# A linear-attention and feed-forward kernel: products with the state row-tiled over two PSUM banks, the state update issued behind them

## The chip, the cores and the metric

The kernel runs on one core of one Trainium2 chip. The metric is the time of one execution in microseconds (us); of the kernel before there are three runs with a median of 691.35 us (689.48 to 691.96). One more execution was taken with the hardware profiler.

## The reference

Three stages follow one another; everything is float32.

```python
# 1 attention with a decaying state: batch 4, 8 heads, 768 steps, head size 48
for t in range(S):
    state = alpha[:, :, t, :, None] * state + np.einsum('bhd,bhe->bhde', k[:, :, t], v[:, :, t])
    y[:, :, t] = np.einsum('bhd,bhde->bhe', q[:, :, t], state)
x = y.transpose(0, 2, 1, 3).reshape(B, S, 384)
# 2 gated feed-forward with a convolution of three taps over time: 384 -> 1024 -> 384
h = np.maximum(x @ w_in, 0.0)
conv_out = conv_w[0] * h[t - 1] + conv_w[1] * h[t] + conv_w[2] * h[t + 1]
x = (h * sigmoid(conv_out)) @ w_out
# 3 layer norm and feed-forward with a residual: 384 -> 1536 -> 384
xn = (x - mu) / np.sqrt(var + 1e-06) * g_ln
out = x + np.maximum(xn @ w_ch1, 0.0) @ w_ch2
```

## The kernel before, in words

Time is cut into 24 chunks of 128 steps (six to a batch, chunks 0, 6, 12 and 18 begin one) and 12 blocks of 256 steps (two chunks each). A chunk is the unit of stage 1, a block that of stages 2 and 3.

**A chunk.** The eight heads stand in four pairs p; the first head of a pair (g = 0) lies on SBUF partitions 0 to 47, the second (g = 1) on 64 to 111 (`rows`). The decays are turned into running products on VectorE (lines 399 and 415), and `a` holds q times the decay, `later` k times its inverse. TensorE (PE) then makes, in this order:

- the scores `s` of all heads (line 441), two PSUM banks, one for each g; the two g work in different halves of the array's rows. VectorE masks them into `pm` (line 450, twice).
- `kt`, four transposes of k (line 465), one bank; ScalarE copies it to `kts` (line 469). The last chunk of a batch leaves `kt` and the update out.
- the outputs `y` (line 509), one bank with four strips of 32 partitions and three column ranges k of 128 steps. The products with the state come first (12, and none in a batch's first chunk), then 16 products of v with `pm`. Each output is 32 features wide, so that four products with four strips stand side by side. In the products with the state (`state[:, p, ...]`, all 112 partitions) both heads of a pair are in the rows: 8 products give the first 32 features of a head (k = 0 and 1), 4 the last 16 of both heads (k = 2).
- the update `u` (line 525), a step of its own with a bank of its own: 8 products of 64 or 48 columns, which VectorE adds to `state` (lines 534 and 536). GpSimd multiplies the state by its decay before the next chunk (line 482).

`evict_x` empties `y`: ScalarE rounds it into `xh` (line 556, one instruction of 128x384) and VectorE writes the rest `xl` (line 562, one instruction). The feed-forward stages work on such pairs of a rounded part and a rest: three products for each one of the reference, at lines 595 (`h`, stage 2, from `xh`, `xl`), 790 (`h`, stage 3) and 687 (`acc`, the second product of both).

**Order.** All instructions are recorded as steps with an estimated cost, and a planner (`Plan.order`) simulates the five engines' queues with these costs, the buffers' rings and due times, and emits the steps in the order that comes out; every engine then runs its list in order. In the first 150 us the weights are converted too (lines 254 to 312: from 64-bit floats, by ScalarE, VectorE, then PE or GpSimd; the tiles `z`, `w`, `low`). From chunk 3 on, all of a chunk's banks come from one ring of two (`att_bank`, tag `att`); chunks 0 to 2 use another ring of three (`acc`).

At the end the kernel reads a flag and, where some decay was out of range, would run a general version (`general`, `general_x`); it isn't run with these inputs.

Of the kernel before, what the change touches and what calls it, by code (L numbers as in the profile page):

```python
# [26 lines left out]
K1 = DM // 128  # L27
# [189 lines left out]
def attn_moe_kernel(ctx: ExitStack, tc, qka, vv, qka_t, v_t, w_in, conv_w, w_out, g_ln, w_ch1, w_ch2, out):  # L217
    nc = tc.nc
    pe, act, dve, pool, sp = nc.tensor, nc.scalar, nc.vector, nc.gpsimd, nc.sync
    plan = Plan()  # L220
    add, ring = plan.add, plan.ring
# [253 lines left out]
    def att_pe2(c):  # L475


        u, t = att[c], {}
        first, last = c % NCB == 0, c % NCB == NCB - 1
        if not first:  # L480
            def decay():
                pool.tensor_tensor(
                    out=state, in0=state,
                    in1=ends[:, c].rearrange("r (p o) -> r p o", o=1).to_broadcast([R, NP, 2 * D]), op=ALU.mult,
                )

            add("pool", pool_us(NP * 2 * D), decay, r=[("ends", c)], w=[("state", 0)], port=True)
        b0 = att_bank(c)

        def outputs():  # L490
            qd, v, pm = prep[c]["qd"], vraw[c], post[c][0]
            ps = t["y"] = bank(b0[0], "y")
            products = []
            if not first:
                for k in range(2):
                    for n in range(4):
                        p, g = divmod(4 * k + n, 2)
                        products.append((k, n, state[:, p, state_mains[g]], qd[:, NP - 1 - p, :]))
                for p in range(NP):
                    products.append((2, p, state[:, p, 32:64], qd[:, NP - 1 - p, :]))  # L500
            for k in range(2):
                for n in range(4):
                    p, g = divmod(4 * k + n, 2)
                    products.append((k, n, v[:, p, mains[g]], pm[:, g, p, :]))
            for g in range(2):
                for p in range(NP):
                    products.append((2, p, v[:, p, rests[g]], pm[:, g, p, :]))
            for m, (k, n, l, r) in enumerate(products):
                pe.matmul(  # L509
                    out=ps[32 * n:32 * n + 32, k * C:(k + 1) * C], lhsT=l, rhs=r,  # L510
                    start=m < 4, stop=m >= len(products) - 4, skip_group_check=True,
                )

        reads = [u["v"], u["pm"], u["a"]] + ([] if first else [("state", 0)])
        add("pe", 0.9 if first else 1.5, outputs, r=reads, new=[b0[1]], mode="cols")
        evict_x(c, t, b0[1])
        if last:
            return
        b1 = att_bank(c)

        def update():
            ps, kts, v = bank(b1[0], "u"), post[c][1], vraw[c]
            for p in range(NP):
                for g, w in enumerate(wide):
                    pe.matmul(  # L525
                        out=ps[w, p * D:(p + 1) * D], lhsT=kts[:, p, w], rhs=v[:, p, wholes[g]], start=True, stop=True,
                    )
            t["u"] = ps[:, :NP * D].rearrange("r (p e) -> r p e", p=NP)

        def add_up():  # L530
            for g, r in enumerate(rows):
                st = state[r, :, blocks[g]]
                if first:
                    dve.tensor_copy(out=st, in_=t["u"][r])
                else:
                    dve.tensor_tensor(out=st, in0=t["u"][r], in1=st, op=ALU.add)

        add("pe", 0.4, update, r=[u["kts"], u["v"]], new=[b1[1]], mode="halves")
        add("dve", 2 * dve_us(NP * D), add_up, r=[b1[1]], w=[("state", 0)])

    def evict_x(c, t, b):

        i, half = divmod(c, NT)
        first, last = i % (S // T) == 0, i % (S // T) == S // T - 1
        new = half == 0
        if new:
            x_b[i] = [ring(f"x{s}", XB) for s in "hl"]
        cols = slice(1 + half * C, 1 + (half + 1) * C)

        def source():  # L550
            return t["y"][:, :DM].rearrange("f (k t) -> f k t", k=K1)

        def high():
            if new:
                x_t[i] = [wk.tile([128, K1, T + 2], F32R, tag="xh", name="xh", bufs=XB), None]
            act.activation(out=x_t[i][0][:, :, cols], in_=source(), func=ACTF.Copy)

        def rest():
            if new:
                x_t[i][1] = wk.tile([128, K1, T + 2], F32R, tag="xl", name="xl", bufs=XB)  # L560
            hi, lo = x_t[i]
            dve.tensor_tensor(out=lo[:, :, cols], in0=source(), in1=hi[:, :, cols], op=ALU.subtract)

        def sides():
            for n, x in enumerate(x_t[i]):
                if new and first:
                    pool.memset(x[:, :, 0:1].bitcast(F32), 0.0)
                if new and not first:
                    before = x_t[i - 1][n]
                    pool.tensor_copy(out=x[:, :, 0:1], in_=before[:, :, T:T + 1])  # L570
                    pool.tensor_copy(out=before[:, :, T + 1:T + 2], in_=x[:, :, 1:2])
                if half == NT - 1 and last:
                    pool.memset(x[:, :, T + 1:T + 2].bitcast(F32), 0.0)

        bh, bl = x_b[i]
        add("act", act_us(DM), high, r=[b], **{"new" if new else "w": [bh]})
        add("dve", dve_us(DM), rest, r=[b, bh], **{"new" if new else "w": [bl]})
        if new or (half == NT - 1 and last):
            add("pool", 0.3, sides, w=[bh, bl] + (x_b[i - 1] if new and not first else []))

# [317 lines left out]
    def general_x(xs, b, t0):  # L898

        hi, lo = x_t[0] = [wk.tile([128, K1, T + 2], F32R, tag=f"x{s}", name=f"x{s}", bufs=1) for s in "hl"]  # L900
        for t, n in [(t, 128) for t in range(0, T, 128)] + [(T, 2)]:
            rowf = wk.tile([128, DM], F32, tag="row", name="row")
            split = 32 * H
            src = xs[bass.ds(b, 1), bass.ds(t0 + t, n)].rearrange("o t g (p e) -> (o t) g p e", e=D)
            for part, es in ((rowf[:n, :split], slice(0, 32)), (rowf[:n, split:], slice(32, D))):
                for g in range(2):
                    sp.dma_start(
                        out=part.rearrange("t (p g e) -> t p g e", p=NP, g=2)[:, :, g, :], in_=src[:, g, :, es]
                    )
            ps = psum.tile([128, 512], F32, tag="h", name="h", bufs=HB)  # L910
            for k in range(K1):
                pe.transpose(ps[:, k * 128:k * 128 + n], rowf[:n, k * 128:(k + 1) * 128], ident[:n, :n])
            src = ps[:, :DM].rearrange("p (k t) -> p k t", k=K1)[:, :, :n]
            act.activation(out=hi[:, :, t:t + n], in_=src, func=ACTF.Copy)
            dve.tensor_tensor(out=lo[:, :, t:t + n], in0=src, in1=hi[:, :, t:t + n], op=ALU.subtract)
# [35 lines left out]
    begin, n = {}, 0  # L951
# [75 lines left out]
    for s, i, part in up:  # L1027
        m = begin[s, i, part]
# [61 lines left out]
def _layout(inputs):  # L1090
# [34 lines left out]
    for n in ("moe_w_in", "moe2_w_ch1"):  # L1125
        w = inputs[n]
        if n == "moe_w_in":
            w = w.reshape(H, D, -1)
            w = np.concatenate([w[:, :32].reshape(32 * H, -1), w[:, 32:].reshape(DM - 32 * H, -1)])
        w = w.reshape(K1, 128, -1, 128)  # L1130
        weights[n] = w.transpose(2, 1, 0, 3).reshape(-1, 128, DM)
    for n in ("moe_w_out", "moe2_w_ch2"):
# [25 lines left out]
```

## Time and profile before

| | us |
|---|---|
| median of three runs | 691.35 |
| the profiled execution | 688.87 |
| its span, first to last instruction | 687.1 |
| PE busy (matmul) | 643.6 |
| VectorE (DVE) busy | 449.5 |
| ScalarE (ACT) busy | 308.8 |
| GpSimd (POOL) busy | 127.1 |

PE is the engine that is busy in nearly all of the span. A matmul of float32 operands leaves two records in the trace, one of the rounded operands (`fp32r`) one. [...] PEclk is the clock granted to PE, 1.00 for 2.4 GHz and 0.50 for 1.2 GHz.

### The profile page before, as it was taken

How to read it: one execution, taken by the hardware profiler on the slowest of the kernel's cores; microseconds unless marked ns; L12 is line 12 of the kernel's file. 1: busy time of each engine (PE TensorE's matmuls, PEld its weight loads, DVE VectorE, ACT ScalarE, POOL GpSimd, SP SyncE). 2: the span in 40 equal slices, each digit the busy share in tenths (PEclk: the TensorE clock that was granted, in tenths of full speed). 3: DMA queues.
4: the chain of work that ended last, by engine and by line, in shares of the span. 5: the costliest groups of instructions: out<-in, count | busy, mean ns of one | idle time of the engine just before them, and what ended most of it. 6: DMA issues, size and time to landing. Idle time of an engine off the chain costs nothing.

```text
span 687.1 us, 14178 instructions
## 1 busy us (share of the span) xinstructions
PE 643.6 (94%) x5754; PEld 609.2 (89%) x5754; DVE 449.5 (65%) x902; ACT 308.8 (45%) x752; POOL 127.1 (19%) x193
## 2 busy tenths in 40 slices
PE   3779868889999999999999999999999999999995
PEld 2557858789999999999999999999999999999994
DVE  5989998989749549639549548648648547365221
ACT  2758775445436336335335335345245245253210
POOL 4143244451320121201111111201201100000000
PEclk9999998979999999999999999999999999999998
DMA  9999101012310211110120111110100000000000
GB/s 303 307 359 298 55 0 42 16 41 79 98 56 24 58 57 39 57 42 24 56 56 25 57 57 44 57 37 30 55 14 24 18 1 24 1 24 1 2 24 27
DMA packets 15738, 44.51 MB, mean 65 GB/s; under 512 B 1473, under 2 KB 4673, under 8 KB 15665
## 3 DMA queue, kind: packets, MB, share of 16 engines
q1 hardware_dynamic: 15664, 43.52, 20.1%
q8 instruction: 47, 0.77, 0.5%
q14 instruction: 27, 0.21, 0.1%
HBM read 38.80 MB, written 4.72 MB: 63 GB/s over the span
## 4 chain that ended last, share of the span: by engine, by line
PE 83%; DVE 8%; ACT 3%; issue 2%; DMA 1%; POOL 1%; SPq 0%; ACTq 0%; DVEq 0%
PE acc L687 34%; PE h L790 22%; PE h L595 14%; PE y L509 5%; PE s L441 4%; DVE z L260 2%; DVE z L263 2%; PE u L525 2%; PE h L756 1%; DVE cv L616 1%; DMA raw<-in_qka 1%; PE kt L465 1%; DVE gl L661 1%; DVE z L257 1%; PE low L305 1%
## 5 line engine op out<-in xcount | busy, mean ns | idle before, releaser
L687 PE MATMUL acc<-w,gh 128*128 128x384 f32 x960 | 254.7, 346 | 3.0 <-ACT w L301 1.5
L687 PEld LDWEIGHTS acc<-w,gh 128*128 128x128 f32 x960 | 163.2, 190 | 7.3 <-ACT w L301 1.7
L687 PE MATMUL acc<-w,gl 128*128 128x384 f32 x480 | 162.5, 339 | 0.1
L803 DVE SCALAR_TENSOR_TENSOR gl<-h,gh 128x256 fp32r<-128x256 f32 x144 | 60.7, 423 | 153.7 <-ACT gh L798 153.0
L798 ACT ACTIVATE gh<-h 128x256 fp32r<-128x256 f32 x144 | 55.2, 384 | 195.9 <-PE acc L687 184.5
L790 PE MATMUL h<-xnh,w 128*128 128x256 f32 x864 | 129.2, 285 | 1.5 <-POOL w L312 1.5
L790 PEld LDWEIGHTS h<-xnh,w 128*128 128x128 f32 x864 | 119.4, 190 | 3.3 <-POOL w L312 1.8
L616 DVE SCALAR_TENSOR_TENSOR cv<-h,cw,cv 128x256 f32<-128x256 f32 x192 | 91.8, 481 | 28.8 <-ACT cv L612 24.4
L687 PEld LDWEIGHTS acc<-w,gl 128*128 128x128 f32 x480 | 91.1, 190 | 0.7 <-DVE gl L803 0.7
L595 PE MATMUL h<-xh,w 128*128 128x258 f32 x576 | 86.9, 286 | 4.7 <-DVE gl L661 2.9
L595 PEld LDWEIGHTS h<-xh,w 128*128 128x128 f32 x576 | 78.2, 189 | 8.8 <-DVE gl L661 4.8
L790 PE MATMUL h<-xnl,w 128*128 128x256 f32 x432 | 75.3, 283 | 0.0
L790 PEld LDWEIGHTS h<-xnl,w 128*128 128x128 f32 x432 | 62.2, 190 | 0.0
L635 ACT ACTIVATE cv<-cv 128x256 f32<-128x256 f32 x96 | 39.7, 415 | 37.1 <-DVE cv L616 36.8
L608 ACT ACTIVATE h<-h 128x258 f32<-128x258 f32 x96 | 35.5, 370 | 46.0 <-PE h L595 45.5
L402 POOL COPY ends<-later 112x4 f32<-112x4 f32 x24 | 4.9, 203 | 261.1 <-DVE later L399 259.5
L595 PE MATMUL h<-xl,w 128*128 128x258 f32 x288 | 50.1, 282 | 0.0
L612 ACT ACTIVATE cv<-h,cw 128x256 f32<-128x256 f32 x96 | 45.5, 474 | 1.9
L639 DVE TENSOR_TENSOR h<-h,cv 128x256 f32<-128x256 f32 x96 | 40.5, 424 | 5.9 <-ACT cv L635 4.0
L661 DVE TENSOR_TENSOR gl<-h,gh 128x256 fp32r<-128x256 f32 x96 | 40.1, 417 | 5.6 <-ACT gh L656 5.2
L656 ACT ACTIVATE gh<-h 128x256 fp32r<-128x256 f32 x96 | 36.7, 383 | 10.3 <-DVE h L639 9.1
L595 PEld LDWEIGHTS h<-xl,w 128*128 128x128 f32 x288 | 41.3, 190 | 0.0
(87 smaller groups left out, 742.6 us busy)
## 6 DMA issues: line engine op xcount, KB each, us to landing
raw<-in_qka SPq DMA_DIRECT2D x23, 673.8 KB, 4.8
w<-in_moe_w_ch SPq DMA_DIRECT2D x12, 768.0 KB, 16.5
vraw<-in_vv SPq DMA_DIRECT2D x24, 256.0 KB, 2.8
out<-x SPq DMA_DIRECT2D x11, 384.0 KB, 2.5
w<-in_moe_w_in SPq DMA_DIRECT2D x4, 768.0 KB, 11.4
w<-in_moe_w_out SPq DMA_DIRECT2D x4, 768.0 KB, 13.5
raw<-in_qka SPq DMA_DIRECT2D x1, 448.0 KB, 3.8
out<-x SPq DMA_DIRECT2D x2, 192.0 KB, 3.3
```

The costliest lines, as they stand in the source:

```text
L595: pe.matmul(out=ps[:, :T + 2], lhsT=w1[j][:, l, k * 128:(k + 1) * 128], rhs=r[:, k, :], start=n == 0, stop=n == 3 * K1 - 1,)
L608: act.activation(out=t["h"], in_=t["h"], func=ACTF.Relu)
L612: act.activation(out=t["cv"], in_=t["h"][:, 0:T], func=ACTF.Copy, scale=cw[:, 0, j:j + 1])
L616: dve.scalar_tensor_tensor(out=t["cv"], in0=t["h"][:, k:k + T], scalar=cw[:, k, j:j + 1], in1=t["cv"], op0=ALU.mult, op1=ALU.add,)
L635: act.activation(out=t["cv"], in_=t["cv"], func=ACTF.Sigmoid)
L639: engine.tensor_tensor(out=g, in0=g, in1=t["cv"], op=ALU.mult)
L656: act.activation(out=m_t[0, i, j][0], in_=t["h"][:, 1:T + 1], func=ACTF.Copy)
L661: engine.tensor_tensor(out=lo, in0=t["h"][:, 1:T + 1], in1=hi, op=ALU.subtract)
L687: pe.matmul(out=acc_t[s, i][t][:, :DM], lhsT=l[:, ts], rhs=w[j][:, r], start=j in firsts and n == 0, stop=j + 1 in lasts and n == 2,)
L790: pe.matmul(out=ps[:, :T], lhsT=w3[j][:, l, k * 128:(k + 1) * 128], rhs=r[:, k, :], start=n == 0, stop=n == 3 * K1 - 1,)
L798: act.activation(out=m_t[1, i, j][0], in_=u["ps"][:, :T], func=ACTF.Relu)
L803: dve.scalar_tensor_tensor(out=lo, in0=u["ps"][:, :T], scalar=0.0, in1=hi, op0=ALU.max, op1=ALU.subtract)
```

## The change

The outputs of a chunk now take two banks (`t["y"]` is a list). `place(k)` puts column range k = 0 and 2 into the first, k = 1 into the second. The eight products for the first 32 features are made of one head each: g = 0 with rows 0 to 47 into the first bank, g = 1 with rows 64 to 111 into the second, in turn; strip n is now the pair p. The four products for the last 16 features keep all 112 rows. The update is recorded in the same step, right behind the outputs, and writes into the second bank's columns from 128 on. `evict_x` takes two instructions each on ScalarE and VectorE: 128x2x128 from the first bank and 128x128 from the second. The features' order in x changes, and so the rows of `w_in` are permuted on the host, and the general version's loads.

```diff
-        b0 = att_bank(c)
+        b0, b1 = att_bank(c), att_bank(c)
+        def place(k):
+            return t["y"][k % 2][:, (k // 2) * C:(k // 2 + 1) * C]
 
         def outputs():
             qd, v, pm = prep[c]["qd"], vraw[c], post[c][0]
-            ps = t["y"] = bank(b0[0], "y")
+            t["y"] = [bank(b[0], "y") for b in (b0, b1)]
             products = []
             if not first:
-                for k in range(2):
-                    for n in range(4):
-                        p, g = divmod(4 * k + n, 2)
-                        products.append((k, n, state[:, p, state_mains[g]], qd[:, NP - 1 - p, :]))
+                for p in range(NP):
+                    for g, r in enumerate(rows):
+                        products.append((g, p, state[r, p, state_mains[g]], qd[r, NP - 1 - p, :]))
                 for p in range(NP):
                     products.append((2, p, state[:, p, 32:64], qd[:, NP - 1 - p, :]))
...
                 pe.matmul(
-                    out=ps[32 * n:32 * n + 32, k * C:(k + 1) * C], lhsT=l, rhs=r,
...
+                    out=place(k)[32 * n:32 * n + 32], lhsT=l, rhs=r,
...
-        add("pe", 0.9 if first else 1.5, outputs, r=reads, new=[b0[1]], mode="cols")
-        evict_x(c, t, b0[1])
...
         def update():
-            ps, kts, v = bank(b1[0], "u"), post[c][1], vraw[c]
+            kts, v = post[c][1], vraw[c]
+            ps = t["y"][1][:, C:]
...
-        add("pe", 0.4, update, r=[u["kts"], u["v"]], new=[b1[1]], mode="halves")
-        add("dve", 2 * dve_us(NP * D), add_up, r=[b1[1]], w=[("state", 0)])
...
+        def products():
+            outputs()
+            if not last:
+                update()
+        reads = [u["v"], u["pm"], u["a"]] + ([] if first else [("state", 0)]) + ([] if last else [u["kts"]])
+        us = (0.9 if first else 1.3) + (0 if last else 0.5)
+        add("pe", us, products, r=reads, new=[b0[1], b1[1]], mode="cols")
+        evict_x(c, t, (b0[1], b1[1]))
+        if not last:
+            add("dve", 2 * dve_us(NP * D), add_up, r=[b1[1]], w=[("state", 0)])
...
+        def tiles():
+            yield slice(0, K1, 2), t["y"][0][:, :2 * C].rearrange("f (k t) -> f k t", k=2)
+            yield slice(1, 2), t["y"][1][:, :C].rearrange("f (k t) -> f k t", k=1)
...
-            act.activation(out=x_t[i][0][:, :, cols], in_=source(), func=ACTF.Copy)
+            for ks, ps in tiles():
+                act.activation(out=x_t[i][0][:, ks, cols], in_=ps, func=ACTF.Copy)
...
-            dve.tensor_tensor(out=lo[:, :, cols], in0=source(), in1=hi[:, :, cols], op=ALU.subtract)
+            for ks, ps in tiles():
+                dve.tensor_tensor(out=lo[:, ks, cols], in0=ps, in1=hi[:, ks, cols], op=ALU.subtract)
```

Since steps and costs differ, the planner's order differs in many places. Three are shown. The first is PE at the outputs of chunk 23, the last one; the numbers behind a name tell the buffers apart. Before:

```order
L687 MATMUL acc_6893<-w2_1_331,gh_6901 128x384 x2
L687 MATMUL acc_6893<-w2_1_331,gl_6915 128x384
L509 MATMUL y_6947<-a_6415,state_80 32x128 x12
L509 MATMUL y_6947<-pm_6860,vraw_6522 32x128 x16
L595 MATMUL h_6983<-xh_6004,w1_3_524 128x258 x6
```

One bank takes the twelve products with the state and the sixteen with `pm`. Now, on PE at the same chunk:

```order
L512 MATMUL y_6895<-a_6460,state_80 32x128
L512 MATMUL y_6896<-a_6460,state_80 32x128
L512 MATMUL y_6895<-a_6460,state_80 32x128
L512 MATMUL y_6896<-a_6460,state_80 32x128
L512 MATMUL y_6895<-a_6460,state_80 32x128
L512 MATMUL y_6896<-a_6460,state_80 32x128
L512 MATMUL y_6895<-a_6460,state_80 32x128
L512 MATMUL y_6896<-a_6460,state_80 32x128
L512 MATMUL y_6895<-a_6460,state_80 32x128 x4
L512 MATMUL y_6895<-pm_6661,vraw_6322 32x128 x4
L512 MATMUL y_6896<-pm_6661,vraw_6322 32x128 x4
L512 MATMUL y_6895<-pm_6661,vraw_6322 32x128 x8
```

Eight products go to two banks in turn, and only behind them come those that use all rows. The second place is PE at chunk 12, which begins a batch and so has no products with the state. Before:

```order
L509 MATMUL y<-pm,vraw 32x128 x16
L687 MATMUL acc<-w_0_829,gh 128x384 x2
L687 MATMUL acc<-w_0_829,gl 128x384
L687 MATMUL acc<-w_0_829,gh 128x384 x2
L687 MATMUL acc<-w_0_829,gl 128x384
L790 MATMUL h<-xnh,w_2_1110 128x256 x6
L790 MATMUL h<-xnl,w_2_1110 128x256 x3
L687 MATMUL acc<-w_0_829,gh 128x384 x2
L687 MATMUL acc<-w_0_829,gl 128x384
L687 MATMUL acc<-w_0_829,gh 128x384 x2
L687 MATMUL acc<-w_0_829,gl 128x384
L525 MATMUL u<-vraw,kts 64x48
```

The update stood three steps of the feed-forward behind the outputs. Now, on PE at the same chunk:

```order
L512 MATMUL y<-pm,vraw 32x128 x16
L524 MATMUL y<-vraw,kts 64x48
L524 MATMUL y<-vraw,kts 48x48
L524 MATMUL y<-vraw,kts 64x48
L524 MATMUL y<-vraw,kts 48x48
L524 MATMUL y<-vraw,kts 64x48
L524 MATMUL y<-vraw,kts 48x48
L524 MATMUL y<-vraw,kts 64x48
L524 MATMUL y<-vraw,kts 48x48
```

It stands right behind them. Over the whole list, 9 of the 20 updates stood alone before (those of chunks 6, 7, 9, 12, 13, 15, 18, 19 and 21); now none does. The third place is VectorE in the first 50 us, from the second mask of chunk 2 past that chunk's `xl`. Before:

```order
L450 TENSOR_TENSOR pm<-s,mask 128x512
L260 SCALAR_TENSOR_TENSOR z<-w_2_156,z 128x768
L263 SCALAR_TENSOR_TENSOR z<-w_2_156,z 128x768
L399 SCALAR_TENSOR_TENSOR later<-raw,from_one 112x516
L536 TENSOR_TENSOR state<-u,state 48x4x48 x2
L562 TENSOR_TENSOR xl<-y,xh 128x3x128
L405 RECIPROCAL from_end<-later 112x4
L415 SCALAR_TENSOR_TENSOR a<-raw,from_end 112x516
```

Now, on VectorE from the first mask of the same chunk to its `xl`:

```order
L450 TENSOR_TENSOR pm<-s,mask 128x512
L260 SCALAR_TENSOR_TENSOR z<-w_3_122,z 128x768
L263 SCALAR_TENSOR_TENSOR z<-w_3_122,z 128x768
L450 TENSOR_TENSOR pm<-s,mask 128x512
L260 SCALAR_TENSOR_TENSOR z<-w_2_156,z 128x768
L263 SCALAR_TENSOR_TENSOR z<-w_2_156,z 128x768
L405 RECIPROCAL from_end<-later 112x4
L415 SCALAR_TENSOR_TENSOR a<-raw,from_end 112x516
L536 TENSOR_TENSOR state<-y,state 48x4x48 x2
L575 TENSOR_TENSOR xl<-y,xh 128x2x128
L575 TENSOR_TENSOR xl<-y,xh 128x128
```

The rest `xl` of chunk 2 has moved behind two instructions of another weight's conversion (`z<-w_3_122`) and the scan `a` of chunk 3, and it is two instructions.

## Rows read from the trace of the kernel before

**Rows 1.** Busy time of each engine by stretch: bounds in us, length, busy (records).

```profile
20.00:60.00 40.00, 30.19 (x263) 21.21 (x263) 35.24 (x53) 27.82 (x55) 9.53 (x12) 0.91 1.03 334
60.00:147.20 87.20, 72.73 (x624) 66.60 (x621) 79.96 (x135) 48.68 (x103) 38.31 (x33) 0.90 0.16 47
147.20:678.70 531.50, 531.45 (x4786) 514.19 (x4784) 321.00 (x699) 225.52 (x584) 71.03 (x123) 1.00 0.13 38
```

**Rows 2.** PE's waits: who waited for whom, us in total, times, longest.

```profile
PE h L756 <- DVE gl L661: 6.2, 1, 6.2
...
PE h L790 <- POOL w L312: 1.5, 1, 1.5
```

**Rows 3.** PE in order of time at chunk 22: start us, us, operation.

```profile
545.59 0.51 PE L790 MATMUL h<-xnl,w 128*128 128x256 f32 x3
546.03 0.86 PE L509 MATMUL y<-a,state 112*32 112x128 f32 x24
546.71 1.06 PE L509 MATMUL y<-pm,vraw 128*32 128x128 f32 x32
547.70 0.67 PE L525 MATMUL u<-vraw,kts 128*64 128x48 f32 x16
548.29 0.61 PE L687 MATMUL acc<-w,gh 128*128 128x384 f32 x2
```

**Rows 4.** The lines of the outputs in three short windows of chunk 22: PE busy (records).

```profile
546.02:546.06 0.04, 0.03 (x4) 1.00 0.00 0
546.02:546.13 0.11, 0.10 (x4) 1.00 0.00 0
546.15:546.23 0.08, 0.08 (x8) 1.00 0.00 0
```

**Rows 5.** PE in order of time at chunk 22's scores.

```profile
542.23 1.16 PE L441 MATMUL s<-a,later 48*128 48x128 f32 x16
543.32 0.61 PE L687 MATMUL acc<-w,gh 128*128 128x384 f32 x2
```

**Rows 6.** PE in order of time around an update that stands alone (chunk 21).

```profile
536.75 0.51 PE L790 MATMUL h<-xnl,w 128*128 128x256 f32 x3
...
537.79 0.61 PE L687 MATMUL acc<-w,gh 128*128 128x384 f32 x2
538.24 0.34 PE L687 MATMUL acc<-w,gl 128*128 128x384 f32 x1
...
539.65 0.52 PE L790 MATMUL h<-xnl,w 128*128 128x256 f32 x3
540.01 0.51 PE L687 MATMUL acc<-w,gh 128*128 128x384 f32 x2
540.36 0.34 PE L687 MATMUL acc<-w,gl 128*128 128x384 f32 x1
```

**Rows 7.** PE in order of time at chunk 23, which has no update.

```profile
574.50 1.05 PE L509 MATMUL y<-pm,vraw 128*32 128x128 f32 x32
575.48 0.98 PE L595 MATMUL h<-xh,w 128*128 128x258 f32 x6
```

**Rows 8.** Groups of VectorE and ScalarE: operation xcount, busy us, mean ns, idle before.

```profile
L661 DVE TENSOR_TENSOR gl<-h,gh 128x256 fp32r<-128x256 f32 x96 | 40.1, 417 | 5.6 <-ACT gh L656 5.2
...
L562 DVE TENSOR_TENSOR xl<-y,xh 128x384 fp32r<-128x384 f32 x24 | 13.1, 548 | 3.5 <-ACT xh L556 3.4
```

**Rows 9.** VectorE in order of time after chunk 2's update; in brackets what it waited for.

```profile
42.72 0.72 DVE L536 TENSOR_TENSOR state<-u,state 48x192 f32<-48x192 f32 x2 [0.41 <-PE u L525]
...
44.16 1.38 DVE L415 TENSOR_TENSOR_SCAN a<-raw,from_end 112x516 f32<-112x516 f32 x1
...
48.51 1.00 DVE L616 SCALAR_TENSOR_TENSOR cv<-h,cw,cv 128x256 f32<-128x256 f32 x2 [2.53 <-ACT cv L612]
```

**Rows 10.** PE alone in the stretch before 147.2: length, busy (records), granted clock.

```profile
137.00:147.20 10.20, 7.85 (x29) 0.50 0.00 0
```

**Rows 11.** PE in order of time at its last wait for a weight.

```profile
143.88 1.01 PE L790 MATMUL h<-xnh,w 128*128 128x256 f32 x3 [1.46 <-POOL w L312]
```

More of the change, by code (lines that the diff above doesn't have):

```diff
@@ L487, in att_pe2 @@
             add("pool", pool_us(NP * 2 * D), decay, r=[("ends", c)], w=[("state", 0)], port=True)
-        b0 = att_bank(c)
+        b0, b1 = att_bank(c), att_bank(c)
+        def place(k):
+            return t["y"][k % 2][:, (k // 2) * C:(k // 2 + 1) * C]
         def outputs():
             qd, v, pm = prep[c]["qd"], vraw[c], post[c][0]
-            ps = t["y"] = bank(b0[0], "y")
+            t["y"] = [bank(b[0], "y") for b in (b0, b1)]
             products = []
             if not first:
-                for k in range(2):
-                    for n in range(4):
-                        p, g = divmod(4 * k + n, 2)
-                        products.append((k, n, state[:, p, state_mains[g]], qd[:, NP - 1 - p, :]))
+                for p in range(NP):
+                    for g, r in enumerate(rows):
+                        products.append((g, p, state[r, p, state_mains[g]], qd[r, NP - 1 - p, :]))
                 for p in range(NP):
                     products.append((2, p, state[:, p, 32:64], qd[:, NP - 1 - p, :]))
[L501 to L504, printed above, removed]
+            for g in range(2):
+                for p in range(NP):
+                    products.append((g, p, v[:, p, mains[g]], pm[:, g, p, :]))
             for g in range(2):
@@ L507, in outputs @@
                     products.append((2, p, v[:, p, rests[g]], pm[:, g, p, :]))
+            begun = set()
             for m, (k, n, l, r) in enumerate(products):
                 pe.matmul(
-                    out=ps[32 * n:32 * n + 32, k * C:(k + 1) * C], lhsT=l, rhs=r,
-                    start=m < 4, stop=m >= len(products) - 4, skip_group_check=True,
-                )
-        reads = [u["v"], u["pm"], u["a"]] + ([] if first else [("state", 0)])
-        add("pe", 0.9 if first else 1.5, outputs, r=reads, new=[b0[1]], mode="cols")
-        evict_x(c, t, b0[1])
-        if last:
-            return
-        b1 = att_bank(c)
+                    out=place(k)[32 * n:32 * n + 32], lhsT=l, rhs=r,
+                    start=(k % 2, n) not in begun, stop=(k % 2, n) not in [(q[0] % 2, q[1]) for q in products[m + 1:]],
+                    skip_group_check=True,
+                )
+                begun.add((k % 2, n))
         def update():
-            ps, kts, v = bank(b1[0], "u"), post[c][1], vraw[c]
+            kts, v = post[c][1], vraw[c]
+            ps = t["y"][1][:, C:]
             for p in range(NP):
@@ L526, in update @@
                         out=ps[w, p * D:(p + 1) * D], lhsT=kts[:, p, w], rhs=v[:, p, wholes[g]], start=True, stop=True,
+                        skip_group_check=True,
                     )
@@ L536, in add_up, with evict_x @@
                     dve.tensor_tensor(out=st, in0=t["u"][r], in1=st, op=ALU.add)
-        add("pe", 0.4, update, r=[u["kts"], u["v"]], new=[b1[1]], mode="halves")
-        add("dve", 2 * dve_us(NP * D), add_up, r=[b1[1]], w=[("state", 0)])
-    def evict_x(c, t, b):
+        def products():
[8 more added lines that the diff above has]
+            add("dve", 2 * dve_us(NP * D), add_up, r=[b1[1]], w=[("state", 0)])
+    def evict_x(c, t, banks):
         i, half = divmod(c, NT)
@@ L548, in evict_x @@
         cols = slice(1 + half * C, 1 + (half + 1) * C)
-        def source():
-            return t["y"][:, :DM].rearrange("f (k t) -> f k t", k=K1)
+        def tiles():
+            yield slice(0, K1, 2), t["y"][0][:, :2 * C].rearrange("f (k t) -> f k t", k=2)
+            yield slice(1, 2), t["y"][1][:, :C].rearrange("f (k t) -> f k t", k=1)
         def high():
@@ L575, in evict_x @@
         bh, bl = x_b[i]
-        add("act", act_us(DM), high, r=[b], **{"new" if new else "w": [bh]})
-        add("dve", dve_us(DM), rest, r=[b, bh], **{"new" if new else "w": [bl]})
+        add("act", act_us(DM) + 0.17, high, r=banks, **{"new" if new else "w": [bh]})
+        add("dve", dve_us(DM) + 0.15, rest, r=[*banks, bh], **{"new" if new else "w": [bl]})
         if new or (half == NT - 1 and last):
@@ L904, in general_x @@
             src = xs[bass.ds(b, 1), bass.ds(t0 + t, n)].rearrange("o t g (p e) -> (o t) g p e", e=D)
[L905 to L909, printed above, removed]
+            for g in range(2):
+                sp.dma_start(
+                    out=rowf[:n, :split].rearrange("t (g p e) -> t g p e", p=NP, g=2)[:, g], in_=src[:, g, :, :32]
+                )
+                sp.dma_start(
+                    out=rowf[:n, split:].rearrange("t (p g e) -> t p g e", p=NP, g=2)[:, :, g, :], in_=src[:, g, :, 32:]
+                )
             ps = psum.tile([128, 512], F32, tag="h", name="h", bufs=HB)
@@ L1128, in _layout @@
             w = w.reshape(H, D, -1)
-            w = np.concatenate([w[:, :32].reshape(32 * H, -1), w[:, 32:].reshape(DM - 32 * H, -1)])
+            w = np.concatenate([w[0::2, :32], w[1::2, :32]]).reshape(32 * H, -1), w[:, 32:].reshape(DM - 32 * H, -1)
+            w = np.concatenate(w)
         w = w.reshape(K1, 128, -1, 128)
```

## The prediction

> **What bounds the kernel now.** I read the busy time by stretch first. From 147.2 to 678.7 us PE is busy for 531.45 of 531.50 us at full clock [rows 1]: no other engine holds it up, and each us less of PE work there is a us less of the whole. Ahead of that it is different. From 60 to 147.2 us PE is busy for 72.7 of 87.2 us and VectorE for 80.0 [rows 1], and the list of PE's waits ends on VectorE (6.2 us in one wait) and on the conversion of weights, which VectorE feeds (1.5 us for a weight from GpSimd) [rows 2]. So in the first 147 us VectorE's list decides, and PE work saved there is worth little. The view in order of time around chunk 22 then gives the prices on PE.
>
> **The products with the state.** Their 24 records take from 546.03 to 546.71, 0.68 us [rows 3]. The short windows show how: four records begin within 0.04 us, no fifth by 0.11, and between 0.13 and 0.21 us eight are under way [rows 4]. So PE takes them in steps of four, one step each 0.11 us: six steps are 0.66, and 0.02 is left for the entry. The 16 products with `pm`, 32 records, are eight steps, 0.88 us, and last 0.99 until the update begins [rows 3]: a change of the array's partition costs about 0.11 us more than staying in one.
>
> Now the eight products of one head each have 16 records. That two halves of the rows work side by side is seen in the scores: 16 records of the same 128 columns take 1.09 us [rows 5], where one after the other at 0.11 they would need 1.76. I take eight at once: two steps, 0.22 us; 0.03 for the later start of the last four, since the first four spread over nearly 0.04 [rows 4]; 0.11 for the change from half rows to all rows, which the kernel before doesn't have; the other four products in two steps, 0.22; and the 0.02. That is 0.60 against 0.68 us, 0.08 saved. Bounds: with a free change of rows it is 0.49, 0.19 saved; if two halves of the rows don't combine with four strips and the eight still go by fours, 4 x 0.11 + 0.11 + 0.22 + 0.02 = 0.79, 0.11 lost. I choose the middle one, because every change of partition in these rows is paid. Of the 20 chunks with a state product, 1 to 5 lie ahead of 147.2 us; 15 count: 15 x 0.08 = 1.2 us saved (2.9 saved to 1.7 lost).
>
> On the change of rows the Trainium skill, TensorEngine Tiling (Array Packing), Key Properties, says that changing the tiling mode, and not just the tile, drains the engine. That speaks for the 0.60 and against the 0.49; the trace agrees for the change from strips of 32 to halves of 64 columns (0.11 us), and doesn't show this one.
>
> **The update behind the outputs.** An update that stands alone: from the last `h` group to the next `acc` 1.04 us (536.75 to 537.79), against 0.36 without one (539.65 to 540.01); and the first two `acc` records take 0.45 instead of 0.35 [rows 6], since PE returns from another partition. Together 0.68 + 0.10 = 0.78 us. Behind the outputs it takes 547.70 to 548.29, 0.59 [rows 3]; the outputs themselves last as long with an update behind them (0.99) as without (0.98 [rows 7]), and the return is paid by them anyhow. So 0.19 us each, for the nine updates that stood alone; the first of them is chunk 6's, behind 147.2 us. 9 x 0.19 = 1.7 us saved. This one rests on the order alone, and I bound it by 1.4 and 2.0 (0.15 to 0.22 each, as the rows are rounded).
>
> **Two instructions for one in the emptying of x.** On VectorE 384 columns cost 548 ns and 256 cost 417 [rows 8], 1.02 ns a column, so 128 cost 286 and the pair 703: 0.155 us more a chunk; on ScalarE about as much, taking its fixed part as like. Behind 147.2 us that is 18 x 0.155 = 2.8 us on VectorE, hidden under PE: VectorE is busy for 321 of 531.5 us [rows 1]. If that cover went, the 2.8 us would be the price. Ahead of it stand six chunks, in VectorE's full stretch: 6 x 0.155 = 0.9 us lost, from 0 (it falls into VectorE's 7.2 idle us of 60 to 147.2 us [rows 1]) to 1.9 (ScalarE's part on the chain too).
>
> **The order of the start.** The planner has rearranged the first 150 us. Ahead of chunk 2's `xl` there is now more of VectorE's work: a pair of conversion steps and the scan of chunk 3, 1.38 us [rows 9] and the rest about as long, so that the first `h` begins some 3 to 4 us later. The work comes off what stood behind it, and the 2.53 us in which VectorE then waited for ScalarE [rows 9] can only be filled or met again. I take 0 for this. What it may cost or give is bounded by that idle time on either side, 2.5 us. The clock adds to it: from 137 to 147.2 us PE ran at 1.2 GHz [rows 10] after its waits for weights. Of this stretch the part behind the last such wait, 143.88 to 147.2 [rows 11], would take half, so 1.7 us, at 2.4 GHz, and as much more elsewhere if PE idles at a new place.
>
> **Sum.** -1.2 - 1.7 + 0.9 + 0 = -2.0 us. The profiled execution, 688.87 us with a span of 687.1, would become 686.9. It lies 2.5 us below the median of the runs, which I take as the base: 691.35 - 2.0 = 689.35, say 689.3 us. A measurement of this kernel can tell about 0.5% from no change, 3.5 us here, so the forecast is within it.
>
> **Rivals.**
>
> Faster by more, from the start: the split's 0.9 us falls into idle time and PE doesn't fall to 1.2 GHz ahead of 147 us. -1.2 - 1.7 - 1.7 = -4.6, so 686.7 us. For it: VectorE has idle time to fill, and the clock's stretch hangs on two waits of 1.5 us. Against: the weights come by the same engines in nearly the same order. Chance 0.2.
>
> The change of rows is free: -2.9 - 1.7 + 0.9 = -3.7, so 687.6 us. Against: each change in [rows 3, 6] is paid. Chance 0.1.
>
> The eight don't go at once (the change doesn't do what it says): +1.7 - 1.7 + 0.9 = +0.9, so 692.2 us, still within 0.5%. For it: no row shows half rows and strips together. Against: halves alone and strips alone both go side by side [rows 4, 5]. Chance 0.1.
>
> A rule that would have a like effect is in the Trainium skill, TensorE: Matmul & The Clock Gate, under "Wait — 56ns, not 53.3ns?": start-to-start never drops below about 25 ns. By it 16 records would take 0.40 us instead of 0.25, and the part with the state 0.75: 15 x 0.07 = 1.0 us lost, 691.5 us in all. The trace doesn't agree: four records begin within 0.04 us [rows 4], so I give it no chance beyond that 0.1.
>
> Slower: the joined step waits, and PE with it. It needs both banks of the ring and `kts`, where the outputs alone needed one bank and no `kts`; and the next scores need both banks emptied by two ScalarE and two VectorE instructions and two additions to the state. All three kinds stand in lists with the feed-forward's work. Behind a joined step that waits, PE's whole list waits. If it or the scores behind it lose 0.5 us in each of the 18 chunks after 147.2 us, 9 us come on top: 691.35 - 2.0 + 9.0 = 698.3 us; it makes the kernel slower by 0.5% from about 0.3 us a chunk. For it: on VectorE the additions and the pieces of `xl` take 0.72 + 0.70 = 1.4 us [rows 8, 9], more than one step of the feed-forward on PE (1.1). Against: in the order at least two such steps stand between a joined step and the next scores, and the kernel before, with as many banks and similar distances, has no wait at all there [rows 1]. Chance 0.1.
>
> **Chances and range.** The forecast itself has 0.5, with a range of its own of 687 to 692 us from the start's order alone. Faster by over 0.5% (below 687.9): 0.15 from the first rival, 0.07 from the second and 0.09 from the forecast's lower edge, 0.31. Slower by over 0.5% (above 694.8): 0.08 from the last and 0.02 from the start, 0.10. Within: 0.59. The range reaches from the first rival's time less 0.7 to the upper end of the third with the start's uncertainty, 686.0 to 693.5 us.
>
> **What would show it.** Right: PE's busy stretch at full clock from about 148 us to the end, shorter by some 2.9 us; the outputs with the state in 0.60 us, sixteen of their records within 0.25; the update right behind in 0.59. Wrong: PE waits in the list behind 148 us, above all at lines of the scores or the outputs; state products in 0.79 us (no eight at once) or 0.49 (free change); or a first wait-free us that has moved by more than 2.5 us, either way.

## The result and the profile after

The changed kernel takes **701.6 us** in the median of five runs (695.05 to 702.14), the kernel before 691.35 (688.70 to 691.96, five runs). The ratio is 1.014, with a 95% interval of 1.0096 to 1.0184: about 10 us slower. The forecast was 689.3 with 686.0 to 693.5, no change; the time lies above the range.

The profiled execution is the quickest of the five, 695.05 us with a span of 693.3; the other four took 701.3 to 702.1. What parts the two is taken up at the experiment *after_again*.

Busy time by stretch in the profile after, answering to [rows 1]; the columns are bounds, length, then PE, PEld, DVE, ACT and POOL (records), PEclk, DMA share, GB/s:

```profile
20.00:60.00 40.00, 30.83 (x248) 19.90 (x246) 32.05 (x47) 23.31 (x45) 8.12 (x12) 0.83 1.03 350
60.00:147.20 87.20, 69.58 (x625) 63.00 (x625) 79.58 (x143) 52.23 (x116) 33.09 (x30) 0.96 0.13 37
147.20:180.00 32.80, 29.64 (x242) 27.92 (x243) 26.37 (x52) 17.09 (x46) 11.26 (x11) 0.90 0.20 62
180.00:678.70 498.70, 498.64 (x4528) 481.22 (x4527) 298.03 (x668) 212.05 (x557) 70.81 (x115) 1.00 0.12 37
```

From 180 us on PE is full at 2.4 GHz, as before. Ahead of that two things differ from [rows 1]. PE's last long wait for a weight ends 7.0 us later than in [rows 11], at 150.84 us where it was 143.88:

```profile
150.84 1.01 PE L803 MATMUL h<-xnh,w 128*128 128x256 f32 x3 [2.69 <-POOL w L312]
```

And between 20 and 60 us VectorE got through 32.05 us of work where it had got through 35.24. It waited more in this pair of profiles; how much of that is the change is taken up at *e3_plan*.

Its waits in the first 62 us, before and after, are (who waited for whom, us in total, times, longest), before:

```profile
DVE cv L616 <- ACT cv L612: 2.5, 1, 2.5
...
DVE z L257 <- ACT z L254: 1.0, 2, 0.5
DVE pm L450 <- PE s L441: 0.4, 1, 0.4
```

and after:

```profile
DVE z L257 <- ACT z L254: 5.3, 5, 2.4
...
DVE pm L450 <- PE s L441: 3.1, 2, 2.7
DVE state L536 <- ACT xh L568: 1.2, 1, 1.2
```

The 2.5 us that I had counted as the only idle time worth filling are gone, and at three other places 9.6 us stand where there had been 1.8 (the addition to the state, L536, had waited 0.4 us for PE). The milestones on PE, as the starts of the same group in the two traces: chunk 1's scores 17.17 and 18.72 us, chunk 2's 35.26 and 40.87, the first `h` of stage 2 46.22 and 53.20 (+7.0), the first transpose of stage 3 104.87 and 111.56 (+6.7), the fifth 200.45 and 209.77 (+9.3), the end of the span 687.1 and 693.3 (+6.2). The fifth transpose needs a correction: chunk 9's scores stand behind it in the kernel before and ahead of it in the changed one. Before:

```profile
207.62 1.16 PE L441 MATMUL s<-a,later 48*128 48x128 f32 x16
```

and after:

```profile
204.36 1.16 PE L441 MATMUL s<-a,later 48*128 48x128 f32 x16
```

They take 1.09 us from their start to that of the next group (207.62 to 208.71; records overlap in these rows, so lengths are read from start to start). So some 8.2 us are lost in the first 200 us, and some 2 are won back in the rest. (The first `h` isn't a measure of the loss either: two more conversion products stand ahead of it in the changed kernel. At the first transpose both kernels have done the same groups on PE.)

The winning back is what the change was reckoned at. PE in order of time at chunk 22 of the profile after, answering to [rows 3] (start us, us, operation):

```profile
538.14 0.33 PE L700 MATMUL acc<-w,gl 128*128 128x384 f32 x1
538.40 0.81 PE L512 MATMUL y<-a,state 48*32 48x128 f32 x24
539.03 1.06 PE L512 MATMUL y<-pm,vraw 128*32 128x128 f32 x32
540.01 0.67 PE L524 MATMUL y<-vraw,kts 128*64 128x48 f32 x16
540.61 0.98 PE L803 MATMUL h<-xnh,w 128*128 128x256 f32 x6
```

The part with the state takes 538.40 to 539.03, 0.63 us, where it took 0.68; the update right behind 0.60. The line of the outputs in two short windows there, answering to [rows 4]; the columns are bounds, length, PE and PEld (records), PEclk, DMA share, GB/s:

```profile
538.40:538.50 0.10, 0.10 (x8) 0.10 (x16) 1.00 0.00 0
538.40:538.65 0.25, 0.24 (x16) 0.18 (x16) 1.00 0.00 0
```

Eight records begin within 0.10 us (four did before), and the sixteen within 0.25: the eight products do go at once.

### The profile page after: what moved, and what is told of

It reads as the page before. It is cut to its first block, busy times and chain, and to the rows that moved or that the text cites. A ratio compares the mean times of both kernels' runs of the same rounds, so it can differ in the third digit from the quotient of the medians.

```text
span 693.3 us, 14299 instructions
## 1 busy us (share of the span) xinstructions
PE 644.1 (93%) x5754; PEld 604.5 (87%) x5754; DVE 449.6 (65%) x926; ACT 312.4 (45%) x776; POOL 131.5 (19%) x193
## 4 chain that ended last, share of the span: by engine, by line
PE 84%; DVE 8%; ACT 2%; issue 2%; POOL 1%; DMA 0%; DVEq 0%; ACTq 0%; POOLq 0%
PE acc L700 34%; PE h L803 22%; PE h L608 14%; PE y L512 5%; PE s L441 4%; DVE z L260 2%; DVE z L263 2%; PE y L524 2%; PE h L769 1%; PE low L305 1%; POOL w L312 1%; PE kt L465 1%; DVE later L399 1%; DVE z L257 1%; DVE cv L629 1%
## 5 line engine op out<-in xcount | busy, mean ns | idle before, releaser
L700 PE MATMUL acc<-w,gh 128*128 128x384 f32 x960 | 251.1, 342 | 2.2 <-POOL w L312 1.5
L608 PE MATMUL h<-xh,w 128*128 128x258 f32 x576 | 88.6, 290 | 4.0 <-DVE gl L674 3.8
L419 POOL TENSOR_TENSOR a<-raw,a 112x512 f32<-112x512 f32 x24 | 29.9, 1246 | 119.0 <-DVE a L415 119.0
L482 POOL TENSOR_TENSOR state<-state,ends 112x384 f32<-112x384 f32 x20 | 19.2, 959 | 124.2 <-PE h L608 81.3
```

The lines of the kernel that those rows point to most:

```text
L608: pe.matmul(out=ps[:, :T + 2], lhsT=w1[j][:, l, k * 128:(k + 1) * 128], rhs=r[:, k, :], start=n == 0, stop=n == 3 * K1 - 1,)
L700: pe.matmul(out=acc_t[s, i][t][:, :DM], lhsT=l[:, ts], rhs=w[j][:, r], start=j in firsts and n == 0, stop=j + 1 in lasts and n == 2,)
```

## The experiments

The kernel before was run again beside each batch: 691.17, 691.12 and 691.88 us, 23 runs each. None of these kernels leaves out any of the computation.

**Order or instructions?** *e1_late* has the old manner (one bank, an update of its own, one instruction for each emptying) in chunks 0 to 6 and the new one from chunk 7 on; *e2_early* the reverse.

```diff
+def NEW(c):
+    return c > 6        # e2_early: c <= 6
```

> Chunks 0 to 6 in the manner of before (one bank, products with the state by fours, update a step of its own, one emptying instruction on each engine), chunks 7 to 23 as changed; the order of all engines up to chunk 7's outputs is that of before. If the order of the start is the cause: PE's wait-free stretch begins at about 148 us as before, and is shorter by 15 state parts x 0.06 and 8 updates x 0.2, 2.5 us, so 688.9 us. If the joined step itself makes PE wait later on: no gain, 691 to 700 us, with PE waits behind 150 us.

> The reverse of the first: chunks 0 to 6 as changed, 7 to 23 in the manner of before. If the order of the start is the cause: first h at 52 to 54 us, and 9 us or more lost against the kernel before, 698 to 704 us. If the joined step in the later part is: 691 to 692 us.

*e1_late* took 688.69 us (12 runs), ratio 0.9977 (0.9959 to 0.9995); *e2_early* 701.94 us, ratio 1.0168 (1.0133 to 1.0204). The change is a small gain behind the start and the whole loss inside it.

*e3_plan* has the new instructions in every chunk, but hands them to the planner as the kernel before did:

```diff
-        add("pe", us, products, r=reads, new=[b0[1], b1[1]], mode="cols")
+        add("pe", 0.9 if first else 1.5, outputs, r=reads, new=[b0[1]], mode="cols")
+        evict_x(c, t, (b0[1],))
+        add("pe", 0.4, update, r=[u["kts"], u["v"]], new=[b1[1]], mode="halves")
-        add("act", act_us(DM) + 0.17, high, ...)
+        add("act", act_us(DM), high, ...)
```

> All instructions of the changed kernel (two banks, eight state products in turn, two emptying instructions), but planned with the steps and costs of before, so that PE's order is that of before and the update a step of its own. If the order of the start is the cause: first h at 46 to 47 us, wait-free from 148 to 149 us, 15 x 0.06 saved and at most 0.9 us for the split emptying, so 690.4 to 691.4 us. If the new instructions are the cause (two more for each emptying, two banks held): first h at about 53 us and 695 to 702 us, as with the change.

It took 691.35 us (12 runs), ratio 1.0009 (0.9990 to 1.0027). So the split banks, the split emptying and the products by halves lose nothing that can be told from the runs' scatter (the interval is -0.7 to +1.9 us); the order that the joined step brings about does. In its profile the first `h` stands at 49.0 us, the first transpose at 109.0, the fifth at 204.8.

That also corrects a base. The profiled run of before, with its first `h` at 46.2, was one of its quickest: *e1_late* and *e9_late_again*, which have the same instructions in the same order up to chunk 7, show 50.2 and 48.5. One reason can be read: chunk 1's four `kt` transposes take 0.60 us in the profile of before (at 19.02) and 1.01 in *e9_late_again* (at 20.05), so PE came to its full speed later there. The profiled run of *e3_plan*, 693.29 us, lies 1.9 us above its median. Against it the quick run of the changed kernel is 2.6 us late at the first transpose (111.56), and some 3.8 at the fifth, with chunk 9's scores taken off.

VectorE in *e3_plan*, its busy time by stretch:

```profile
20.00:60.00 40.00, 30.51 (x245) 21.33 (x244) 32.24 (x50) 24.08 (x48) 9.50 (x12) 0.87 1.03 339
```

and its waits in the first 62 us:

```profile
DVE cv L626 <- ACT cv L622: 3.5, 1, 3.5
DVE xl L572 <- ACT xh L565: 2.4, 1, 2.4
...
DVE pm L450 <- PE s L441: 0.9, 1, 0.9
DVE z L257 <- ACT z L254: 0.8, 2, 0.4
```

With the order of before it got through no more there (32.24 us) than in the changed kernel, and it waited 8.2 us in all for other engines, against 9.6: at other places, but not much less. What the quick run of the changed kernel lost against this one shows on PE, whose waits from 55 to 185 us add up to 21.0 us against 17.4. Among the lines that grew, in *e3_plan* (none there for `xl`):

```profile
PE h L800 <- POOL w L312: 1.5, 1, 1.5
...
PE s L441 <- ACT w L309: 0.3, 1, 0.3
```

and in the changed kernel:

```profile
PE h L803 <- POOL w L312: 3.1, 2, 2.7
PE s L441 <- ACT w L309: 1.8, 2, 1.2
PE s L441 <- DVE xl L575: 1.8, 1, 1.8
```

The scores of chunks 3 and 4 and a weight of stage 3 find their inputs late.

*after_again* is the changed kernel once more.

> The changed kernel once more, for a second trace: four of its five runs took 701 to 702 us and one, the profiled, 695. Either theory: 695 to 702 us; if PE's clock is what lies between the two, a trace of 701 us has one more stretch at 1.2 GHz in the first 160 us, and the same durations behind it.

700.79 us (four runs, 699.47 to 701.50), ratio 1.0142 (1.0106 to 1.0177), and a profile of a run at 701.14, where the first one was of the quick 695.05. PE in order of time at chunk 3's scores, in the quick run:

```profile
61.13 0.48 PE L441 MATMUL s<-a,later 48*128 48x128 f32 x2 [1.22 <-ACT w L309]
62.24 1.16 PE L441 MATMUL s<-a,later 48*128 48x128 f32 x14 [0.63 <-ACT w L309]
63.33 0.99 PE L608 MATMUL h<-xh,w 128*128 128x258 f32 x6
```

and in the other:

```profile
62.99 0.48 PE L441 MATMUL s<-a,later 48*128 48x128 f32 x2 [1.21 <-ACT w L309]
64.10 2.07 PE L441 MATMUL s<-a,later 48*128 48x128 f32 x14 [0.62 <-ACT w L309]
66.10 1.66 PE L608 MATMUL h<-xh,w 128*128 128x258 f32 x6
```

The waits are alike to 0.01 us (in brackets); behind them the same products take 1.16 us in one run and 2.07 in the other. The stretches from 63 and from 77 us (columns as in the first view), in the quick run:

```profile
63.00:71.00 8.00, 7.47 (x112) 6.53 (x108) 6.35 (x13) 5.80 (x15) 3.24 (x4) 1.00 0.07 23
77.00:81.00 4.00, 4.00 (x85) 3.30 (x84) 3.32 (x7) 2.20 (x5) 0.27 (x1) 1.00 0.00 0
```

and in the other:

```profile
63.00:71.00 8.00, 7.38 (x38) 6.87 (x39) 6.33 (x15) 5.16 (x12) 3.16 (x3) 0.57 0.54 146
77.00:81.00 4.00, 4.00 (x26) 3.78 (x27) 3.50 (x9) 0.80 (x2) 0.35 (x1) 0.57 0.70 220
```

In these stretches PE ran at 2.4 GHz throughout in the one, and mostly at 1.2 (mean granted clock 0.57) in the other. The lag of the second run against the first grows from 1.9 us at the first `h` (55.07 and 53.20) to 6.3 at the first transpose (117.84 and 111.56), and is 6.1 at the end. So behind waits of the same length the clock fell in one execution and not in the other, and that makes 4.4 of the 6 us between 695 and 701. The other 1.9 us were there at the first `h` already.

**Which join?** All four kernels have the new instructions everywhere; the update is recorded in one step with the outputs only in the chunks named, elsewhere with the two steps of before.

```diff
+def JOIN(c):
+    return c == 0   # e4_join0; e5_join_but0: c > 0; e7_join3: c > 2; e6_joinlate: c > 6
```

> All instructions are the changed kernel's; only chunk 0's update is recorded in one step with its outputs (and only its emptying has the higher cost), all later chunks have the planner's steps of before. That alone makes the planner put a weight's conversion product ahead of chunk 1's scores and, on VectorE, another weight's conversion and chunk 3's scans ahead of chunk 2's masks and xl, as in the changed kernel. Theory (that order, from the first conversion product on, is the loss): the first h 7 to 9 us later than with the order of before, 697 to 702 us. Rival 1 (the loss comes from the joined steps of chunks 1 to 6, whose wait for kts or for a second bank holds PE up): 690 to 692 us. Rival 2 (half the loss from each): 694 to 697 us.

> The counterpart: every chunk but chunk 0 has the joined step, chunk 0 has the two steps of before. PE's order is then that of before up to chunk 2's outputs; behind them it differs (another conversion product ahead of them, chunk 2's xl behind one more weight's conversion on VectorE). Theory (the conversion ahead of chunk 1's scores begins the loss): 690 to 693 us, the first h within 2 us of that of the kernel with the planner's steps of before. Rival 1 (joined steps of chunks 1 to 6): 697 to 702 us. Rival 2 (half from chunk 2's rearrangement): 694 to 697 us.

> All chunks have the new instructions (two banks, eight products at once, emptying in two pieces); joined steps only from chunk 7 on, so that the order up to chunk 7's outputs is that of before. Theory (the order of the start is the whole loss, the new instructions cost nothing there): 688.2 to 689.5 us, as with the old manner in chunks 0 to 6 (688.69) or a little less. Rival (the new instructions cost 0.9 to 1.9 us in VectorE's full stretch, as the emptying's second pieces do): 689.6 to 690.6 us.

> As the last one, but joined steps already from chunk 3 on: the order of before up to chunk 3's scores, then another one in the stretch from 55 to 150 us. Theory (what is lost is lost ahead of the first h): 688 to 690.5 us. Rival (a joined step anywhere in the weights' conversion, up to 150 us, loses): 692 to 700 us.

Measured, with the earlier kernels between them (the starts are those of each profiled run, in us; at the first transpose PE has done the same groups in all of them, while the last three kernels of the table have two more conversion products ahead of the first `h`):

| joined in chunks | kernel | median us | ratio to before (95%) | first `h` | first transpose |
|---|---|---|---|---|---|
| none | e3_plan | 691.35 | 1.0009 (0.9990 to 1.0027) | 49.0 | 109.0 |
| 7 and on | e6_joinlate | 690.14 | 0.9989 (0.9972 to 1.0007) | 48.6 | 108.6 |
| 3 and on | e7_join3 | 692.18 | 1.0024 (1.0009 to 1.0039) | 49.4 | 109.2 |
| 1 and on | e5_join_but0 | 695.93 | 1.0082 (1.0058 to 1.0105) | 49.2 | 109.6 |
| all | after_again | 700.79 | 1.0142 (1.0106 to 1.0177) | 55.1 | 117.8 |
| 0 alone | e4_join0 | 698.27 | 1.0123 (1.0091 to 1.0156) | 53.4 | 114.6 |

My theory for this batch, that everything begins with the conversion ahead of chunk 1's scores, held half: *e4_join0* fell in its range, *e5_join_but0* did not (3 us above it, in the range of the rival that gives half the loss to chunk 2's rearrangement), and *e7_join3* was 1.7 us above it and at the lower edge of the rival's. *e6_joinlate* fell in its rival's range too; the last batch comes back to that. Down the ladder each step ahead of chunk 7 costs: joining chunks 3 to 6 some 2.0 us, chunks 1 and 2 3.8, chunk 0 4.9; joining from 7 on gains 1.2. The two places don't add up, though: chunk 0 alone costs 6.9 us against *e3_plan*, the others without it 4.6, both together 9.4.

What the kernels above 695 us share can be read. Chunk 3's scores wait for a converted weight's emptying in all of them (*after*, *e2_early*, *e4_join0*, *e5_join_but0* and the next one, *e8_cost0*): 1.2 to 1.3 us and then 0.6 to 0.8; in *e7_join3* and *e3_plan* such a wait is 0.3 in all. *e4_join0* shows the half clock behind it in its profile (those 14 records take 2.07 us again). In *e5_join_but0* the times themselves fall into two groups, four runs at 692.7 to 694.6 and four at 697.2 to 697.5, and the mean granted clock of each run goes with them: 0.977 to 0.982 in the first group, 0.971 to 0.974 in the second. Where the second group lost its clock isn't shown, as the one profile there is of this kernel is of the first.

**One number.** *e8_cost0* is the changed kernel with nothing but the planner's cost of chunk 0's joined step changed.

```diff
-        us = (0.9 if first else 1.3) + (0 if last else 0.5)
+        us = 0.9 if c == 0 else (0.9 if first else 1.3) + (0 if last else 0.5)
```

> The changed kernel with one number of the planner changed: chunk 0's joined step is reckoned at 0.9 us instead of 1.4. Every step stays joined, every instruction is the same; with that number the planner leaves chunk 1's scores ahead of the first conversion product, and PE's whole order is that of the kernel in which chunk 0 alone kept two steps. Theory (the order alone decides): the time of that kernel, 695.9, so 694 to 697.5 us, some 5 us under the changed kernel. Rival (the joined step of chunk 0 costs by itself, whatever stands behind it): 700 to 702 us.

695.98 us (six runs, 693.21 to 697.21), ratio 1.0071 (1.0047 to 1.0094), as the theory had it: some 5 us from a number that changes no instruction, only where they stand. What that number does can be seen on PE at 15 to 20 us, in the changed kernel (columns as above):

```profile
15.27 1.09 PE L524 MATMUL y<-vraw,kts 128*64 128x48 f32 x16
16.82 1.65 PE L305 MATMUL low<-z,ident 128*128 128x384 f32 x2 [0.46 <-DVE z L263]
17.76 1.03 PE L306 MATMUL low<-w,minus 128*128 128x384 f32 x1
18.72 2.08 PE L441 MATMUL s<-a,later 48*128 48x128 f32 x16
```

and in *e8_cost0*:

```profile
15.65 1.09 PE L524 MATMUL y<-vraw,kts 128*64 128x48 f32 x16
16.67 0.79 PE L441 MATMUL s<-a,later 48*128 48x128 f32 x2
17.63 2.07 PE L441 MATMUL s<-a,later 48*128 48x128 f32 x14 [0.16 <-DVE xl L575]
```

The planner lets a bank's emptying begin when the step that filled it ends. With the update in that step it ends 0.5 us later in the plan, so chunk 1's scores get their bank later, and a conversion product, reckoned at 0.9 us, is put into the gap. On the chip ScalarE empties the first bank as soon as the outputs are there (from 15.40 us, while the update runs). Where the scores go first, in *e8_cost0*, they start at 16.67 and, all but two records, at 17.63; here the conversion takes 16.82 to 18.72, 1.9 us, behind a wait of 0.46, and they start at 18.72. VectorE at that place in the changed kernel:

```profile
16.72 0.72 DVE L534 COPY state<-y 48x192 f32<-48x192 f32 x2
17.48 0.62 DVE L575 TENSOR_TENSOR xl<-y,xh 128x256 fp32r<-128x256 f32 x2
20.83 0.69 DVE L450 TENSOR_TENSOR pm<-s,mask 128x512 f32<-128x512 f32 x1 [2.73 <-PE s L441]
```

It stands 2.73 us at the mask, with the conversions behind it in its list. In *e8_cost0* it stands there 0.93 us:

```profile
19.32 1.29 DVE L450 TENSOR_TENSOR pm<-s,mask 128x512 f32<-128x512 f32 x2 [0.93 <-PE s L441]
```

The lag is then handed on: ScalarE gets the next weight's bits later, and VectorE waits for it five times (5.3 us; two times and 0.7 in *e8_cost0*).

**Do the new instructions cost anything in the start?** *e9_late_again* and *e10_joinlate_again* are *e1_late* and *e6_joinlate* once more, side by side.

> The old manner in chunks 0 to 6, the new one from chunk 7 on, once more (688.69 in an earlier comparison), now beside the kernel that has the new instructions in all chunks and joined steps from chunk 7 on (690.14). Theory (new instructions cost nothing in the start): both within 0.5 us of each other, 689 to 690. Rival (they cost VectorE 0.9 to 1.9 us there): this one 688.3 to 689.2, the other one 1.0 to 1.9 us above it.

> New instructions in all chunks, joined steps from chunk 7 on (690.14 in an earlier comparison). Theory (new instructions cost nothing in the start): 689 to 690 us, within 0.5 us of the kernel with the old manner in chunks 0 to 6. Rival (they cost VectorE 0.9 to 1.9 us there): 689.5 to 690.8, 1.0 to 1.9 us above it.

688.95 us, ratio 0.9962 (0.9946 to 0.9978), and 688.20 us, ratio 0.9964 (0.9947 to 0.9981), 12 runs each. Both lie just below the 689 to 690 that I expected. The ratios are alike and the medians 0.75 us apart, a little more than I had allowed, with the new instructions on the quicker side. The rival with 0.9 to 1.9 us lost is not borne out, but its lower end isn't excluded: the first batches had them 1.4 us apart the other way (688.69 and 690.14), and the intervals are some 1 us wide on either side. Both beat the kernel before by 0.1 to 0.4% (ratios 0.9989 to 0.9962 over two comparisons of each; the interval of the 0.9989 takes in 1), and the changed kernel by 1.5 to 1.8%. In busy time by stretch of *e10_joinlate_again*, PE is nearly full from 147.2 us and full from 180:

```profile
147.20:180.00 32.80, 31.89 (x326) 29.82 (x326) 27.91 (x56) 18.36 (x50) 11.23 (x13) 0.94 0.21 64
180.00:678.70 498.70, 498.65 (x4468) 481.14 (x4468) 295.81 (x662) 210.20 (x554) 68.83 (x112) 1.00 0.12 37
```

## Why the prediction was wrong

**The failed step is "the order of the start", taken at 0 and bounded by 2.5 us either side.** It measures about +9.4 us (*after_again* against *e3_plan*, the new instructions with the joined and with the old order), and with the gain of the joined steps from chunk 7 on taken out, 10.7: 4.9, 3.8 and 2.0 in the ladder. Three things in its working were wrong:

- "The work comes off what stood behind it" takes VectorE's list for a sum of work. It is a queue in order: a mask that waits for scores (2.73 us instead of 0.93) holds up the conversions behind it, whose lag ScalarE and PE meet later. I saw VectorE's rearranged list and did not look at PE's, where one product had passed chunk 1's scores.
- The bound was VectorE's idle time before. That bounds what can be filled, not what can be added; the waits at the three places after stand 7.8 us above those at the same places before, and 7.6 above *e3_plan*'s, where 2.5 was the bound. They aren't the loss itself, since *e3_plan* has 5.9 us at places where the changed kernel has none: in the quick run the loss came out in PE's waits behind 55 us, 3.6 us more of them.
- For the clock I allowed 1.7 us, and as much more if PE idled at a new place, but neither entered the sum. In the second of the two profiled runs of the changed kernel the half clock costs 4.4 us between the first `h` and the first transpose (the lag's growth from 1.9 to 6.3), behind a wait that the kernel before hadn't.

**The split, +0.9 us ahead of 147 us, can't be told from 0.** Its price was right: the two pieces on VectorE take 422 and 281 ns (means of 24 in the profile after), the forecast's 703 in all.

```profile
L575 DVE TENSOR_TENSOR xl<-y,xh 128x256 fp32r<-128x256 f32 x24 | 10.1, 422 | 0.5
L575 DVE TENSOR_TENSOR xl<-y,xh 128x128 fp32r<-128x128 f32 x24 | 6.7, 281 | 0.0
```

*e10_joinlate_again* is level with *e9_late_again*. But *e3_plan* is level with before although it has the gain of the products with the state, 0.7 us, so it leaves room for as much lost. Whether the 0.155 us a chunk fall into idle time isn't shown.

**The products with the state** were right in kind and nearly in size. The eight go at once, the change of rows is paid (the part is 0.63, the middle value 0.60, the free change 0.49), and the saving is 0.05 us for 0.08. In *e3_plan*, which has only this gain behind the start and the order of before, the distance to before falls from 4.4 us at the fifth transpose to 3.7 at chunk 22's update: 0.7 us.

**The update right behind the outputs** takes 0.60 against the forecast 0.59. The whole steady gain is best read where the start has the order of before: in *e10_joinlate_again* the third transpose starts 4.1 us behind that of before (151.37 and 147.23) and the last product on PE 1.35 (679.78 and 678.43), so 2.8 us are won, where 2.9 were forecast behind 147.2. PE's waits behind the start, a sign to look for, did not come: 498.64 of 498.70 us from 180 us on. What should have shown the loss did: the first us without waits moved by 7.0 us (143.88 to 150.84), far more than 2.5.

**The rivals.** The slower one, joined steps that wait, gave 698.3 us, near the truth, but for another reason: it set its price behind 147.2 us, where PE is full. Ahead of that, one wait of its kind stands in both profiles of the changed kernel: chunk 4's scores wait 1.76 us for `xl`. The rivals of the state's part fell with the 0.63. Nothing in the list had the planner's order as its mechanism, though the order was at hand; that is where the 0.10 for slower was too little.

Open: how much of each step of the ladder is waiting and how much the clock. The profiles of single runs can't part these, as the same waits come with either clock. The mean granted clock of each run gives a hint: *e5_join_but0*'s first group has that of *e7_join3* (0.977 to 0.982, and 0.978 to 0.985) and lies 1.4 us above it, its second group 5.2 us above it at 0.971 to 0.974. The changed kernel is at 0.967 to 0.973, its one quick run at 0.977. Open as well: for chunks 1 to 6 no run parts the new order from the joined steps' own waits, such as that for `xl`; *e8_cost0* does so for chunk 0 alone.

## What to carry to other kernels

When a change alters what a list planner is told, cost its new order as an edit of its own: follow each engine's list through the stretch that is short of slack, and ask of every instruction that moved forward whether its inputs are there and who stands behind it in line. Idle time in the old trace is no bound on a loss there. And a kernel whose steady part gains from a change can keep the gain by leaving the start's steps as they were: here that turned 1.4% slower into 0.1 to 0.4% faster.

## What the runs showed that I had not expected

One program has two lengths some 6 us apart, and 4.4 us of it go with whether PE falls to 1.2 GHz behind a wait of the same length (63 to 71 us, mean granted clock 1.00 or 0.57). And in the first 24 us the clock column is no guide. This is the stretch of the conversion ahead of chunk 1's scores, in the profile after:

```profile
16.00:24.00 8.00, 7.54 (x60) 4.79 (x60) 5.19 (x10) 2.99 (x6) 0.91 (x3) 1.00 1.05 380
```

It shows 1.00, but the scores within it last 2.08 us, like the 2.07 of *after_again* at 64.10, where the column fell; at full clock they last 1.16 [rows 5]. I go by the records: PE was at half speed there.
